# GpSimd's scatters spaced in the plan, first fetches on its queue, ten result tiles: a polysketch attention with a top-2 router on one core

## The chip, the cores and the metric

One core of a Trainium2 chip runs the whole kernel in one launch. The metric is the device time of that launch in microseconds (us). "TensorE" (PE in the profile) multiplies matrices, "VectorE" (DVE), "ScalarE" (ACT) and "GpSimd" (POOL) work on elements, "SyncE" (SP) only issues transfers. Every engine runs its own list of instructions in order and waits on semaphores for the others.

## What is computed

Everything is float32. q, k and v have 4 batches, 4 heads, 1088 tokens and 32 values a head; S1 and S2 are 8 x 32 sketches. phi(x) is the outer product of two sketches of x, 64 features:

```python
def phi(x):
    a = np.einsum('rd,bhsd->bhsr', S1, x)
    b = np.einsum('rd,bhsd->bhsr', S2, x)
    return np.einsum('bhsi,bhsj->bhsij', a, b).reshape(*x.shape[:-1], r * r)
q_p, k_p = (phi(q), phi(k))
kv = np.einsum('bhsf,bhsd->bhfd', k_p, v)
z = np.sum(k_p, axis=2)
num = np.einsum('bhsf,bhfd->bhsd', q_p, kv)
den = np.einsum('bhsf,bhf->bhs', q_p, z)[..., None] + 1e-06
attn = num / den
```

The attention's result is read as x, 4352 tokens of 128 values, and goes through a router with 8 experts:

```python
noisy_logits = x @ w_gate + np.log1p(np.exp(x @ w_noise)) * noise
top2 = np.argpartition(-noisy_logits, 2, axis=1)[:, :2]
top2_w = softmax over the two chosen logits
for e in range(8):
    for k in range(2):
        mask = top2[:, k] == e
        h = np.maximum(x[mask] @ w1[e], 0.0)      # w1[e]: 128 x 1024
        out[mask] += top2_w[mask, k, None] * (h @ w2[e])   # w2[e]: 1024 x 128
```

## The kernel before, in words

**A plan orders everything.** Every step is a `Job` in a `Plan`: an engine (or a choice of ScalarE and VectorE), an estimated cost, what it reads and writes, a priority and, for a transfer, a size. `Plan.order()` (L86) is a greedy list scheduler that simulates the engines and, of the jobs that can start soonest (within `SOON`), takes the one with the lowest priority number. `Plan.write()` (L150) emits the jobs in that order. So the plan's times only decide the *order* of each engine's list; on the chip the engines run their lists as fast as the real waits let them. A tile tag has so many buffers (`tag(name, bufs, ...)`), and a job that opens a new buffer waits, in the plan and on the chip, for the users of the one that it replaces. A job with `paced` starts in the plan no sooner than 7.0 us (`SPAN`) after the fifth paced job before it (`BURST`).

**Attention.** For each batch b, `load_kq` and `load_v` issue the loads on SyncE; `turned` transposes k and q on VectorE into kT and qT (L549, L551); `features` multiplies them with the sketches on TensorE (L571), then ScalarE or VectorE copies the low part (lo), VectorE adds it (ab, L590) and forms the outer products phk and phq (L605). GpSimd copies v into vaug (L618, L621). TensorE sums k features times v (L642). `queries` transposes phq on TensorE (L687), copies that to pT, multiplies with the folded weights (L698), and VectorE divides (den, L713; x, L705) and sums the gates' logits. kT, qT, vld, phk, phq and vaug have one buffer each, kq two.

**Router.** It works in five waves: wave 0 is the first four chunks of 128 tokens of b = 0, wave 1 the rest of b = 0, and waves 2, 3, 4 are b = 1, 2, 3. VectorE chooses the experts, counts on TensorE give every token its place, VectorE weighs the rows with their gate into xg (L915), and GpSimd scatters each chunk with an indirect transfer into the table xs in DRAM (L778, out `xs`, 129 values a row: 128 of x and the number of the pair): 8 scatters in wave 0, 10 in wave 1, 18 in each later wave. Between two scatters of one kind `pool_scatter` sets a one-element memset (L776). The table's unused rows are cleared in nine transfers on SyncE (`xs<-pad`).

**Blocks.** 48 blocks u follow, each with one expert and 128 rows (n = 1) or 256 (n = 2) of the table. The first three (`DIRECT`) get their rows by a product with one-hot tiles `oh` (L973). The next five (u < 8, `QUICK`) fetch xb on ScalarE's queue and are transposed by TensorE; the later ones fetch xb in four pieces and the pair numbers ix on SyncE, and VectorE transposes (bT, L1005). A block needs all scatters of its wave and of the one before. Then TensorE multiplies with w1 into hp (L1015, two buffers), ScalarE makes h = relu(hp) (L1023), TensorE multiplies with w2 into acc (L1030), ScalarE or VectorE copies that to `y` (five buffers), and GpSimd scatters y to the table `pairs` (L778, out `pairs`), at places read from first_at, xb or ix. `sums` at last reads both rows of a token from `pairs`, adds them (L1078) and writes out.

**Zero products.** At the end `idle` fills the plan's gaps of TensorE in the first 60 us with products of a tile of zeros, `zb` (L1247).

The priorities that matter here: TOP is -1000, block products have 1000 + 100u, the router of batch b has some 100 b + 20, and the xs scatters one more than that.

Of the kernel before, what the change touches and what calls it, by code (L numbers as in the profile page):

```python
# [29 lines left out]
class Job:  # L30
    def __init__(self, engines, cost, emit, lat, prio, size):
        self.engines, self.cost, self.emit, self.lat, self.prio, self.size = engines, cost, emit, lat, prio, size
        self.paced = False
        self.deps, self.opens, self.end, self.done = set(), [], None, None


class Plan:
# [6 lines left out]
    BURST, SPAN = 5, 7.0  # L44
# [41 lines left out]
    def order(self):  # L86
        free, done, moved, paced, lanes = {}, [], 0.0, [], []
        left = {j: len(j.deps) for j in self.jobs}
        after = {j: [] for j in self.jobs}
        for j in self.jobs:  # L90
            for d in j.deps:
                after[d].append(j)
        cand = [j for j in self.jobs if not left[j]]
        number = {j: i for i, j in enumerate(self.jobs)}

        def ready(j, e):

            return max((d.end if d.engine == e and d.size is None else d.done for d in j.deps), default=0.0)

        while cand:  # L100
            starts = []
            for j in cand:
                at = 0.0
                for b in j.opens:
                    bufs, _, used = self.tags[b.tag]
                    if b.placed or len(used) < bufs:
                        continue
                    ends = [x.done for x in used[-bufs].users]
                    if None in ends:
                        at = None  # L110
                        break
                    at = max(at, max(ends))
                if at is None:
                    continue
                if j.size is not None:
                    if "SP" in j.engines:
                        at = max(at, moved - self.AHEAD)
                    if len(lanes) >= self.LANES:
                        at = max(at, lanes[-self.LANES])
                if j.paced and len(paced) >= self.BURST:  # L120
                    at = max(at, paced[-self.BURST] + self.SPAN)
                for e in j.engines:
                    starts.append((max(at, free.get(e, 0.0), ready(j, e)), j, e))
            assert starts, [(j.engines, j.prio, [b.tag for b in j.opens]) for j in cand]
            first = min(x[0] for x in starts)
            _, s, _, j, e = min((j.prio, s, number[j], j, e) for s, j, e in starts if s <= first + self.SOON)
            cand.remove(j)
            cost = j.cost[e] if isinstance(j.cost, dict) else j.cost
            j.start, j.end, j.engine = s, s + cost, e
            free[e] = j.end  # L130
            if j.paced:
                paced.append(s)
            j.done = j.end + j.lat + self.SYNC
            if j.size is not None:
                moved = max(moved, j.end + 0.6) + j.size / self.RATE
                j.done = max(j.done, moved + 0.8 if e == "SP" else j.end + 1.4 + 2 * j.size / self.RATE)
                lanes.append(j.done)
            j.opens = [b for b in j.opens if not b.placed]
            for b in j.opens:
                b.placed = True  # L140
                self.tags[b.tag][2].append(b)
            done.append(j)
            for a in after[j]:
                left[a] -= 1
                if not left[a]:
                    cand.append(a)
        assert len(done) == len(self.jobs)
        return done
# [13 lines left out]
def kernel(  # L162
# [27 lines left out]
    C = 8  # L190
# [59 lines left out]
    tag("b2", 2, [P, 4 * H, R])  # L250
# [22 lines left out]
    tag("y", 5, [P, 2 * D])  # L273
    tag("oh", 2, [P, 4, P])
# [23 lines left out]
    ROWS = 1.0  # L298
    LAND = 2.2
# [6 lines left out]
    def dma(q, o, i, r, w, prio, size=0, issue=0.45, after=(), done=None):  # L306

        eng = {"SP": Y, "ACT": A}
# [5 lines left out]
        return add(q, issue, emit, r=r, w=w, prio=prio, lat=LAND, after=after, size=size)  # L314
# [7 lines left out]
    def load_kq(b, which, prio):  # L322
# [3 lines left out]
        dma("SP", lambda: t.t[:], lambda: pairs_of(src[b]), (), [t], prio, size=557e3)  # L326

    def load_v(b, prio, queues=("SP",)):
# [3 lines left out]
        for l in range(4):  # L332
            dma(queues[l % len(queues)], lambda l=l: t.t[32 * l:32 * l + 32, :, 0:C, :].rearrange("p h c d -> p h (c d)"),
                lambda l=l: src[:, :, C * l:C * l + C, :].rearrange("t h c d -> t h (c d)"),
                (), [(t, l)], prio, size=131e3, issue=1.2)
# [69 lines left out]
    def constants():  # L405
# [12 lines left out]
        pool_job(1.2, 4, lambda: G.memset(vaug[:, :, :, DH:2 * DH], 0.0), ["ones_v"])  # L418
# [64 lines left out]

    def decode_job():
# [7 lines left out]
        def turns(e):  # L492
            for i in range(2):
                T.transpose(ps.t[:, 2 * R * i:2 * R * i + 2 * R], shared["s4"][:, i, :, :].rearrange("r h d -> r (h d)"),
                            ident[0:2 * R, 0:2 * R])
# [59 lines left out]
    def features(jobs, prio, whole=False, after=(), first=None):  # L555

# [6 lines left out]
        def emit(e):  # L563
            for i, (xT, t, _) in enumerate(jobs):
                lhsT = xT.t[:, P * t:min(P * t + P, S)]
                if whole:
                    for c in range(2):
                        T.matmul(ps.t[rows, W * i:W * i + W], lhsT=lhsT, rhs=sk[:, c, :, :].rearrange("p h x -> p (h x)"),
                                 start=(c == 0), stop=(c == 1), skip_group_check=True)
                else:  # L570
                    T.matmul(ps.t[rows, 2 * W * i:2 * W * i + 2 * W], lhsT=lhsT,  # L571
                             rhs=sk[:].rearrange("p c h x -> p (c h x)"), start=True, stop=True)
        last = add("PE", n * (0.3 if whole else mm(128)), emit, lat=0.15, r=["sk"] + [(xT, t // 4) for xT, t, _ in jobs],
                   w=[ps], prio=prio if first is None else first, touch=[dst for _, _, dst in jobs], after=after)
        if whole:
            b2 = new("b2")
            add(EV, either(n * H * R), lambda e: copy(
                e, b2.t[rows, 0:n * H, :], ps.t[rows, 0:W * n].rearrange("p (i w r) -> p i w r", w=2, r=R)[:, :, 1, :]),
                r=[ps], w=[b2], prio=prio)

            def factors(i, m, w):
                if w == 0:
                    return ps.t[rows, W * i:W * m].rearrange("p (i w r) -> p i w r", w=2, r=R)[:, :, 0, :]
                return b2.t[rows, H * i:H * m, :]
            source = (ps, b2)
        else:
            lo, ab = new("lo"), new("ab")
            x4 = lambda: ps.t[rows, 0:2 * W * n].rearrange("p (i c y) -> p i c y", i=n, c=2)
            add(EV, either(W * n), lambda e: copy(e, lo.t[rows, 0:n, :], x4()[:, :, 1, :]), r=[ps], w=[lo], prio=prio)
            add("DVE", vec(W * n), lambda e: V.tensor_tensor(  # L590
                out=ab.t[rows, 0:n * H, :, :].rearrange("p (i h) w r -> p i (h w r)", h=H),
                in0=x4()[:, :, 0, :], in1=lo.t[rows, 0:n, :], op=ALU.add), r=[ps, lo], w=[ab], prio=prio)

            def factors(i, m, w):
                return ab.t[rows, H * i:H * m, w, :]
            source = (ab,)
        i = 0
        while i < n:
# [10 lines left out]
            add("DVE", vec(256 * (m - i)), product, r=list(source), w=[(jobs[i][2], jobs[x][1]) for x in range(i, m)], prio=prio)  # L609
# [5 lines left out]
    def keys_values(b, prio, head=False, after=()):  # L615
# [8 lines left out]
        features([(kT, t, pk) for t in range(4)], prio + 1, False, after)  # L624
# [3 lines left out]
        features([(kT, t, pk) for t in range(4, 8)], prio + 2, False, after)  # L628
        if head:
            features([(kT, C, pk)], prio + 3, False, after)  # L630
        else:
            features([(kT, C, pk), (qT, C, pq)], prio + 3, False, after)
        turned(qT, qld, 0, 4, prio + 3)
        features([(qT, t, pq) for t in range(4)], prio + 4, False, after, prio + 2.9)
# [39 lines left out]
        features([(qT, t, pq) for t in range(4, 8)], prio + 6, False, after)  # L674
# [107 lines left out]
    def router(b, t0, n, w, x, lg, prio):  # L782
# [153 lines left out]
        for t in range(n):  # L936
            rows = slice(0, HB if t0 + t == C else P)
            for i in range(2):
# [8 lines left out]
                pair.paced = w > 0  # L947
# [10 lines left out]
    def block(u, w, e, r, n):  # L958
# [5 lines left out]
        if u < DIRECT:  # L964
            oh = new("oh")
# [11 lines left out]
        else:  # L977
# [9 lines left out]
            if u < QUICK:  # L987
                dma("ACT", lambda: xb.t[:, 0:n, :], lambda: rows.rearrange("(c p) x -> p c x", p=P),
                    there, [xb], -10 + u, size=66e3 * n, issue=0.5, done=done)
# [45 lines left out]
        for c in range(n):  # L1035
# [8 lines left out]
            sent = add("POOL", ROWS + 0.3, emit, r=[y, xb if u < QUICK else ix], w=[key], prio=TOP + u, lat=LAND)  # L1044
            sent.paced = True
# [7 lines left out]
    def first_index(prio):  # L1053

        def done(ins):
# [4 lines left out]
        dma("ACT", lambda: first_at[:].unsqueeze(2), lambda: xs_e[0:DIRECT, 0:P, D:XW].rearrange("e p x -> p e x"),  # L1060
            routed[0], ["first_at"], prio, issue=0.5, done=done)
# [176 lines left out]
    began = [None]  # L1238

    def idle(a, b):  # L1240
# [3 lines left out]
        if began[0] is None:  # L1244
            began[0] = tile_now("hp")
        for _ in range(int((b - a - 0.3) * 0.8 / (0.44 if b < 7.5 else 0.22))):
            T.matmul(began[0][:], lhsT=zb[:, 0:P], rhs=zb[:], start=True, stop=True)  # L1247
# [37 lines left out]
```

## Time and profile before

| | us |
|---|---|
| median of three runs | 415.56 (410.94 to 416.64) |
| profiled execution, whole time | 407.02 |
| its span in the trace | 405.3 |
| last matmul ends | 392.3 |
| TensorE busy | 355.4 |
| GpSimd busy | 174.3 |
| VectorE busy | 148.7 |
| ScalarE busy | 137.9 |
| TensorE clock granted, mean | 0.954 |

The profile comes from one execution, 407.02 us long, of which the trace shows 405.3. The page gives busy time by engine, the span in 40 slices, the transfer queues, the chain of work that ended last, and groups of instructions: line, engine, operation, output and inputs, count, busy time, mean of one, and the idle time ahead with the engine that ended it. In a timeline each row has a start, a duration, the engine and the line; in brackets stands how long the engine was idle before it and what released it. `remote` is a release that the trace can't put down to an instruction, `issue` time in which it waited for nothing that the trace shows. "SPq" and "ACTq" are the transfer queues that SyncE and ScalarE issue on.

Runs of matmuls are merged into one row, so that the start of a next row can lie a little ahead of the end of the last.

### The profile page before, as it was taken

The page shows a single profiled execution, that of the slowest core. Times are in us where ns is not written, and L with a number is a line of the kernel's source. Part 1 is how long each engine was busy: PE and PEld are TensorE (multiplying, and loading weights), DVE is VectorE, ACT ScalarE, POOL GpSimd, SP SyncE. Part 2 cuts the span into 40 slices and gives each one's busy share as a digit, 9 for nine tenths or more (in the row PEclk, how much of TensorE's full clock was granted, in tenths as well). Part 3 has the DMA queues.
Part 4 walks back from the last instruction along what each step waited for, and adds up shares of the span by engine and source line. Part 5 has one row for each costly group of instructions (what it writes and reads, how often), then busy time and mean ns, then how long its engine had stood idle before and what let it go on. Part 6 is the DMA issues. An engine that isn't in the chain of part 4 may idle for free.

```text
span 405.3 us, 7333 instructions
## 1 busy us (share of the span) xinstructions
PE 355.4 (88%) x2562; PEld 323.4 (80%) x2562; DVE 148.7 (37%) x559; ACT 137.9 (34%) x284; POOL 174.3 (43%) x333
## 2 busy tenths in 40 slices
PE   7988799369998989857996999999999999999970
PEld 4857689269997988747996898899898998999960
DVE  6687565077884777215770000200000110001101
ACT  1252352124532263112541333433334333333430
POOL 6826203572277647680254566522323224233230
PEclk9999899869999999979997999999999999999995
DMA  6988966744231115411121223622212511115403
GB/s 169 278 275 264 290 193 171 258 145 123 37 71 43 45 37 91 84 49 21 31 57 39 52 59 62 198 46 39 42 26 48 180 30 34 22 27 156 121 12 89
DMA packets 68767, 40.69 MB, mean 100 GB/s; under 512 B 49767, under 2 KB 61193, under 8 KB 68728
## 3 DMA queue, kind: packets, MB, share of 16 engines
q1 hardware_dynamic: 62360, 30.24, 30.5%
q0 software_dynamic: 4608, 8.96, 6.9%
q10 hardware_dynamic: 1760, 1.01, 1.1%
q8 instruction: 21, 0.34, 0.4%
q14 instruction: 18, 0.15, 0.1%
HBM read 24.24 MB, written 16.19 MB: 100 GB/s over the span
## 4 chain that ended last, share of the span: by engine, by line
issue 35%; POOL 24%; PE 23%; DMA 9%; DVE 3%; SPq 3%; ACT 1%; POOLq 1%; another core or an unknown queue 1%; DVEq 0%; ACTq 0%
POOL pairs L778 12%; POOL xs L778 8%; PE hp L1015 6%; PE acc L1030 5%; PE bank L571 4%; DMA kq<-in_k_dram 3%; PE bank L698 3%; SPq L311 3%; DMA xb<-xs 2%; DMA pairs<-y,ix 2%; DMA pr<-pairs 2%; POOL step L776 1%; PE bank L687 1%; PE acc L642 1%; PE bank L642 1%
## 5 line engine op out<-in xcount | busy, mean ns | idle before, releaser
L1030 PE MATMUL acc<-w2s,h 128*128 128x128 f32 x1152 | 154.0, 283 | 6.8 <-ACT h L1023 4.6
L1030 PEld LDWEIGHTS acc<-w2s,h 128*128 128x128 f32 x1152 | 144.4, 194 | 18.7 <-ACT h L1023 9.0
L1015 PE MATMUL hp<-bT,w1s 128*128 128x128 f32 (+1 forms) x768 | 147.4, 334 | 2.6 <-ACT h L1023 1.4
L778 POOL DMA_INDIRECT pairs<-y,ix x64 | 63.1, 987 | 143.3 <-ACT y L304 129.2
L1015 PEld LDWEIGHTS hp<-bT,w1s 128*128 128x128 f32 x768 | 115.3, 195 | 10.9 <-ACT h L1023 1.8
L1023 ACT ACTIVATE h<-hp 128x512 f32<-128x512 f32 x141 | 83.9, 597 | 108.2 <-PE hp L1015 78.9
L778 POOL DMA_INDIRECT xs<-xg,to x72 | 72.5, 1007 | 40.9 <-issue 15.7
L1005 DVE STREAM_TRANSPOSE bT<-xb 128x256 f32<-128x256 f32 (+1 forms) x40 | 15.6, 390 | 138.5 <-PE hp L1015 115.7
L304 ACT COPY y<-acc 128x128 f32<-128x128 f32 (+1 forms) x48 | 15.4, 320 | 65.1 <-PE acc L1030 53.0
L698 PE MATMUL bank<-kvw,pT 128*128 128x98 f32 x144 | 20.1, 290 | 9.0 <-issue 4.9
L698 PEld LDWEIGHTS bank<-kvw,pT 128*128 128x128 f32 x144 | 18.5, 203 | 10.3 <-issue 5.8
L687 PE MATMUL bank<-ident,phq 128*128 128x128 f32 x72 | 11.9, 294 | 12.3 <-DVE phq L605 10.8
L304 ACT COPY pT<-bank 128x512 f32<-128x512 f32 (+1 forms) x18 | 10.0, 562 | 34.0 <-PE bank L687 15.9
L1078 DVE TENSOR_TENSOR o<-pr 128x512 f32<-128x512 f32 (+2 forms) x12 | 6.7, 558 | 36.8 <-DMA pr<-pairs 34.4
L687 PEld LDWEIGHTS bank<-ident,phq 128*128 128x128 f32 x72 | 8.8, 153 | 13.4 <-issue 11.9
L304 ACT COPY lo<-bank 128x256 f32<-128x256 f32 (+2 forms) x21 | 7.1, 337 | 20.1 <-PE bank L571 13.2
L642 PE MATMUL bank<-phk,vaug 128*128 128x128 f32 (+1 forms) x108 | 13.1, 277 | 0.0
L605 DVE TENSOR_TENSOR phq<-ab 128x512 f32<-128x512 f32 (+1 forms) x20 | 12.9, 669 | 0.3
L571 PE MATMUL bank<-sk,kT 128*128 128x128 f32 (+1 forms) x72 | 12.5, 322 | 0.5 <-DVE sk L499 0.5
L642 PEld LDWEIGHTS bank<-phk,vaug 128*128 128x128 f32 (+1 forms) x108 | 12.5, 191 | 0.4
L605 DVE TENSOR_TENSOR phk<-ab 128x512 f32<-128x512 f32 (+1 forms) x20 | 12.6, 646 | 0.3
L571 PE MATMUL bank<-sk,qT 128*128 128x128 f32 (+1 forms) x72 | 11.5, 299 | 0.2 <-issue 0.2
(153 smaller groups left out, 242.8 us busy)
## 6 DMA issues: line engine op xcount, KB each, us to landing
xs<-pad SPq DMA_DIRECT2D x9, 516.0 KB
w1s<-in_moe_w_dram SPq DMA_DIRECT2D x8, 512.0 KB
w2s<-in_moe_w_dram SPq DMA_DIRECT2D x8, 512.0 KB
xb<-xs SPq DMA_DIRECT2D x96, 32.0 KB
pr<-pairs SPq DMA_DIRECT2D x6, 512.0 KB
kq<-in_k_dram SPq DMA_DIRECT2D x4, 544.0 KB
kq<-in_q_dram SPq DMA_DIRECT2D x4, 544.0 KB
vld<-in_v_dram SPq DMA_DIRECT2D x14, 128.0 KB
```

Of the source, the lines that this page charges most:

```text
L304: A.copy(o, i) if e == "ACT" else V.tensor_copy(o, i)
L311: ins = eng[e].dma_start(o(), i())
L571: T.matmul(ps.t[rows, 2 * W * i:2 * W * i + 2 * W], lhsT=lhsT, rhs=sk[:].rearrange("p c h x -> p (c h x)"), start=True, stop=True)
L605: V.tensor_tensor(out=jobs[i][2].t[rows, jobs[i][1]:jobs[m - 1][1] + 1, :, :].rearrange("p c h (i j) -> p (c h) i j", i=R), in0=factors(i, ...
L642: T.matmul(kvp.t[:, P * a:P * a + P], lhsT=va.t[0:K, t, hs, :].rearrange("p h d -> p (h d)"), rhs=pk.t[0:K, t, hs, :].rearrange("p h f -> ...
L687: T.transpose(ps.t[:, c0:c0 + P], pq.t[:, t + i, 2 * a:2 * a + 2, :].rearrange("p h f -> p (h f)"), ident[:])
L698: T.matmul(ps2.t[:, c0:c0 + 2 * YW], lhsT=pT.t[:, P * (2 * i + a):P * (2 * i + a) + P], rhs=kvw.t[:, a, :], start=True, stop=True)
L778: return G.indirect_dma_start(**kw)
L1005: add("DVE", vec(P * n), lambda _: V.transpose(bT.t[:, 0:P * n], flat()), r=[xb], w=[bT], prio=TOP + u)
L1015: T.matmul(hp.t[:, P * n * i:P * n * (i + 1)], lhsT=w1s[:, e, P * (js * g + i):P * (js * g + i + 1)], rhs=bT.t[:, 0:P * n], start=True, st ...
L1023: A.activation(out=h.t[:], in_=hp.t[:], func=AF.Relu)
L1030: T.matmul(acc.t[:, D * c:D * c + D], lhsT=h.t[:, P * (n * i + c):P * (n * i + c + 1)], rhs=w2s[:, e, j, :], start=(j == 0 and c == 0), st ...
```

## The change

1. The plan's `BURST` and `SPAN` go. `paced` is a number: a paced job starts in the plan at least so long after the last paced one, 1.45 us for the scatters of wave 0 and 1.7 us for all others and for the result scatters. `far` marks them: a job on the same engine that depends on one waits in the plan for its landing, not only for its end.
2. The result scatters' priority goes from TOP + u to 400 + 0.01u, which puts them behind the xs scatters of the wave that is routed at that time.
3. The five xb fetches of blocks 3 to 7 and first_at go from ScalarE's queue to GpSimd's. Transfers of GpSimd no longer count among the plan's eight `LANES`.
4. Ten buffers of `y` instead of five. The one-hot tiles `oh` are taken from `o`. An unused branch (`whole`, `b2`) goes.
5. The plan adds `MARGIN`, 6.0 us, to the landing of the loads of k, q and v of batches 2 and 3.
6. Zero products: ten at the start, one between the two transposes of the sketches, one in each later gap before 7.5 us; in the later gaps the share of the gap that they fill goes from 0.8 to 0.85. The memset of vaug's upper half moves ahead on GpSimd.

GpSimd's list, which follows from 1 to 3: 8 scatters of wave 0, the six fetches, 10 scatters of wave 1 (7, the small copy of vaug for b = 2, 3, the large copy), 9 result scatters, 18 of wave 2 (7, a copy, 1, a small copy, 10), 6 results, 18 of wave 3, 4 results, 18 of wave 4, then the results that are left. Before, results stood among the scatters of a wave, two results and three xs scatters in turn, for example. On VectorE the transposes of batch 2's k go behind the phq, den and x of batch 1; on SyncE three pieces of v stand ahead of batch 2's k instead of one, and the five ix loads ahead of batch 3's k. Lines of the changed kernel are 6 to 9 lower than before: the scatters are L772, h is L1017, the w2 products L1024.

```diff
-    BURST, SPAN = 5, 7.0
...
-            return max((d.end if d.engine == e and d.size is None else d.done for d in j.deps), default=0.0)
+            return max((d.end if d.engine == e and d.size is None and not d.far else d.done for d in j.deps), default=0.0)
...
-                    if len(lanes) >= self.LANES:
+                    if "POOL" not in j.engines and len(lanes) >= self.LANES:
                         at = max(at, lanes[-self.LANES])
-                if j.paced and len(paced) >= self.BURST:
-                    at = max(at, paced[-self.BURST] + self.SPAN)
+                if j.paced and paced:
+                    at = max(at, paced[-1] + j.paced)
...
-                lanes.append(j.done)
+                if e != "POOL":
+                    lanes.append(j.done)
+                j.done += j.margin
...
-    tag("y", 5, [P, 2 * D])
-    tag("oh", 2, [P, 4, P])
+    tag("y", 10, [P, 2 * D])
...
+    MARGIN = 6.0
...
-        dma("SP", lambda: t.t[:], lambda: pairs_of(src[b]), (), [t], prio, size=557e3)
+        dma("SP", lambda: t.t[:], lambda: pairs_of(src[b]), (), [t], prio, size=557e3, margin=MARGIN if b > 1 else 0.0)
...
-        pool_job(1.2, 4, lambda: G.memset(vaug[:, :, :, DH:2 * DH], 0.0), ["ones_v"])
+        pool_job(1.2, 0.5, lambda: G.memset(vaug[:, :, :, DH:2 * DH], 0.0), ["ones_v"])
...
             for i in range(2):
+                if i:
+                    T.matmul(warm()[:, 0:2 * P], lhsT=zb[:, 0:P], rhs=zb[:, 0:2 * P], start=True, stop=True)
                 T.transpose(ps.t[:, 2 * R * i:2 * R * i + 2 * R], shared["s4"][:, i, :, :].rearrange("r h d -> r (h d)"),
...
-                pair.paced = w > 0
+                pair.paced, pair.far = 1.45 if w == 0 else 1.7, True
...
-            oh = new("oh")
+            oh = new("o")
...
-                dma("ACT", lambda: xb.t[:, 0:n, :], lambda: rows.rearrange("(c p) x -> p c x", p=P),
-                    there, [xb], -10 + u, size=66e3 * n, issue=0.5, done=done)
+                dma("POOL", lambda: xb.t[:, 0:n, :], lambda: rows.rearrange("(c p) x -> p c x", p=P),
+                    there, [xb], -10 + u, size=66e3 * n, issue=1.0, done=done)
...
-            sent = add("POOL", ROWS + 0.3, emit, r=[y, xb if u < QUICK else ix], w=[key], prio=TOP + u, lat=LAND)
-            sent.paced = True
+            sent = add("POOL", ROWS + 0.3, emit, r=[y, xb if u < QUICK else ix], w=[key], prio=400 + 0.01 * u, lat=LAND)
+            sent.paced, sent.far = 1.7, True
...
-        dma("ACT", lambda: first_at[:].unsqueeze(2), lambda: xs_e[0:DIRECT, 0:P, D:XW].rearrange("e p x -> p e x"),
-            routed[0], ["first_at"], prio, issue=0.5, done=done)
+        dma("POOL", lambda: first_at[:].unsqueeze(2), lambda: xs_e[0:DIRECT, 0:P, D:XW].rearrange("e p x -> p e x"),
+            routed[0], ["first_at"], prio, issue=1.0, done=done)
...
-        for _ in range(int((b - a - 0.3) * 0.8 / (0.44 if b < 7.5 else 0.22))):
-            T.matmul(began[0][:], lhsT=zb[:, 0:P], rhs=zb[:], start=True, stop=True)
+        n = 10 if a == 0 else 1 if b < 7.5 else int((b - a - 0.3) * 0.85 / 0.22)
+        for _ in range(n):
+            T.matmul(warm()[:], lhsT=zb[:, 0:P], rhs=zb[:], start=True, stop=True)
```

## The prediction

> **What bounds the kernel now.** I read the page first, then the chain of waits, then TensorE's timeline around each of its pauses, and last the timelines of the engines that it paused for.
>
> ```profile
> PE 355.4 (88%) x2562; PEld 323.4 (80%) x2562; DVE 148.7 (37%) x559; ACT 137.9 (34%) x284; POOL 174.3 (43%) x333
> issue 35%; POOL 24%; PE 23%; DMA 9%; DVE 3%; SPq 3%; ACT 1%; POOLq 1%; another core or an unknown queue 1%; DVEq 0%; ACTq 0%
> ```
>
> TensorE is busy for 355.4 of 405.3 us, so the other 49.9 us are all that an edit of order can win; part of them is the tail (the last matmul ends at 392.3, 13 us before the end) and the start. The stages differ (columns: stretch, its length, then busy time of TensorE, of its weight loads, VectorE, ScalarE and GpSimd, granted clock, DMA share, GB/s):
>
> ```profile
> 72.00:92.00 20.00, 9.63 (x76) 9.24 (x76) 8.53 (x23) 4.27 (x11) 12.92 (x21) 0.74 0.62 194
> 154.00:187.00 33.00, 25.49 (x171) 22.31 (x170) 11.75 (x32) 7.56 (x16) 22.53 (x37) 0.90 0.37 70
> 208.00:225.00 17.00, 13.89 (x74) 12.28 (x74) 3.98 (x14) 4.50 (x9) 10.07 (x15) 0.80 0.23 52
> 260.00:380.00 120.00, 120.00 (x829) 110.09 (x828) 10.45 (x26) 46.07 (x85) 35.64 (x68) 1.00 0.28 64
> ```
>
> From 260 to 380 TensorE is never idle and at full clock: there the change can win nothing. The loss is before 260, in two kinds of place. The first, in the timelines of TensorE, of VectorE and of SyncE's queue:
>
> ```profile
> 74.24 0.38 PE L687 MATMUL bank<-ident,phq 128*128 128x128 f32 x2
> 84.99 1.09 PE L687 MATMUL bank<-ident,phq 128*128 128x128 f32 x4 [10.37 <-DVE phq L605]
> 85.87 1.92 PE L1015 MATMUL hp<-bT,w1s 128*128 128x128 f32 x8
> ...
> 81.81 1.30 DVE L551 STREAM_TRANSPOSE kT<-kq 128x512 f32<-128x512 f32 x2 [13.52 <-DMA kq<-in_k_dram]
> ...
> 59.30 8.53 SPq L311 DMA_DIRECT2D xs<-pad  x5
> 67.94 1.28 SPq L311 DMA_DIRECT2D vld<-in_v_dram  x1
> 69.31 2.03 SPq L311 DMA_DIRECT2D kq<-in_k_dram  x1
> ```
>
> TensorE stands 10.37 us for phq of batch 1. VectorE could have made it, but ahead of that in its order stand the transposes of batch 2's k, and they wait 13.52 us for a load that SyncE issued only at 69.31, behind five clears; it landed 12.5 us later. After the stop the matmuls run at half speed (eight of L1015 take 1.71 us to the next start, against 0.89 at full clock).
>
> The second kind of place is GpSimd's runs of scatters, here ScalarE, TensorE and GpSimd:
>
> ```profile
> 218.12 0.60 ACT L1023 ACTIVATE h<-hp 128x512 f32<-128x512 f32 x1 [3.70 <-remote]
> ...
> 218.77 2.08 PE L1030 MATMUL acc<-w2s,h 128*128 128x128 f32 x8 [3.11 <-ACT h L1023]
> ...
> 213.29 0.97 POOL L778 DMA_INDIRECT xs<-xg,to  x1 [0.30 <-issue]
> ...
> 215.82 0.96 POOL L778 DMA_INDIRECT xs<-xg,to  x1 [0.23 <-issue]
> ```
>
> The first products of that block ended at 214.77, so ScalarE could have made h then; it began at 218.12, 1.34 us after the seventh scatter of an unbroken run had ended (216.78). Outside such runs the hand-over from hp to h takes 0.04 to 0.10 us; at a fifth scatter it is 0.55, further on in a run 1.3 to 4.7. So long runs of scatters, 1.27 us apart, hold up TensorE's signals. What TensorE lost (idle time, plus the extra of half-clock rows after it): run of 8 from 33.3: 3.8 us; 7 from 115.8: 1.7; 8 from 154.3: 1.1; 13 from 166.8: 9.3; 7 from 208.1: 6.2. Together 22.1 us for 18 scatters past the fifth of their run, 1.23 us each. Runs of five with pauses of 1.8 us between (231 to 257) cost three stops of 0.32 to 0.38, about 1 us.
>
> **Part by part, against the profiled execution's 407.02 us.**
>
> *Later k loads (MARGIN).* The plan now believes that batch 2's k lands 6 us later, and in VectorE's order its transposes go behind batch 1's phq, gates and x. TensorE no longer waits there: between its last transposes of phq C and its first product that needs batch 2's kT stand, priced by the same groups at full clock, 0.44 + 0.89 + 1.31 + 0.44 + 0.89 + 0.11 + 1.79 + 0.87 + 0.87 + 0.89 + 1.76 = 10.3 us, so it arrives there at 74.62 + 10.3 = 84.9. The load itself gets later: two more pieces of v stand ahead of it on SyncE, 1.28 us each by the row above, so it lands at 81.81 + 2.6 = 84.4 at worst; 1.30 us of transposes make 85.7. Left is a stop of 0.8 (0 if the pieces cost the load nothing, 1.5 if VectorE adds 0.7). Half-clock time falls away too: 0.44 + 0.81 + 0.29 = 1.5 us on the rows from 84.99 to 89.19. Sum: -10.4 - 1.5 + 0.8 = **-11.1** (-10.4 to -11.9). Behind the moved transposes VectorE's last den and x of batch 1 wait, and on them the router of wave 1, but by the same 0.8 at most.
>
> *Runs of scatters.* Pacing is a matter of the plan; nothing on GpSimd waits for it. What decides is GpSimd's new order. Result scatters had the first priority and now have one behind the wave's xs scatters. Wave 1: 7 xs, a copy of vaug, 3 xs. Then nine results. Wave 2: 7, a copy, 1, a small copy, 10. Six results. Waves 3 and 4: 18 unbroken each, with four results between. Before, waves 2, 3 and 4 lost 2.3, 10.4 and 7.5 us, together 20.2. Nearest rows for after: wave 2 as a run of 7 (1.7) and one of 8 (3.8), 5.5; wave 3, one run of 18 where there were 8 and 13 with results among them, again 10.4; wave 4 as wave 3. That is 26.3, so +6.1 at this reading; 0 if the waves just keep their 20.2. I take the middle, **+3**: fewer scatters lie in the same stretch, since results go elsewhere. The bounds: all three waves as cheap as wave 2 was, -13.3; above, in waves 3 and 4 everything past the fifth scatter is lost (13 x 1.27 = 16.5 us, and 3 us at half clock as after 217), 9.8 + 2 x 19.5 - 20.2 = +28.6. Deferring results needs the ten y tiles, and frees an ix tile later, and SyncE's xb loads stand behind the ix load; five fetched blocks of about 7.3 us each cover that. Without that cover a late block costs what is missing of the 2 to 3 us of a landing.
>
> *Fetches on GpSimd's queue.* Five xb and first_at leave ScalarE, where they took 0.35 us each and first_at 2.36, with y waiting 2.14 behind it. No plain fetch on GpSimd is in this trace; the nearest rows are ScalarE's 0.35 and GpSimd's own scatters, 0.96 to 1.0 us, and I take the latter, the same engine: 6 us in all. They lie in its own idle time: after the wave's last scatter (42.69 + 0.96) it does nothing until 60.93:
>
> ```profile
> 42.69 0.96 POOL L778 DMA_INDIRECT xs<-xg,to  x1 [0.23 <-issue]
> 49.19 0.22 POOL L908 COPY xg<-pid 128x18 int32<-128x18 int32 x1 [5.54 <-DMA xs<-xg,to]
> ...
> 60.93 1.31 POOL L778 DMA_INDIRECT xs<-xg,to  x1 [11.51 <-DVE xg L915]
> ```
>
> The fetch needs the landing (49.19), and six issues end near 55.2, before 60.93: cost **0**, up to +1 if six issues in a row act like a run of six. If the cover were gone, 6 us would delay wave 1's scatters. The Trainium skill ("SBUF — State Buffer", "SBUF: two separate sides") speaks against it: descriptors of a transfer issued on GpSimd are written by GpSimd, which is locked out while VectorE runs a two-port operation, and its example goes from 620 to 3100 ns. By that rule six issues would take up to 18.6 us, an estimate from that page, end near 68 instead of 55, and make the sum about +7 worse; no row here shows VectorE holding an issue of GpSimd, so I go by the rows.
>
> *Start.* Ten zero products instead of nine (0.447 us each, so the tenth ends at 5.87 beside a transpose that ran at 5.69: +0.2), one more between the two sketch transposes, one or none before 7.5 us, to have the clock up sooner. Sixteen L571 take 3.78 us there against two times 0.89 to 1.06 later. But VectorE and ScalarE carry that stretch: **-0.6** (+0.2 to -0.9). The earlier memset of vaug on GpSimd (1.02 us) delays ident, which is needed only at 5.69: nothing.
>
> *Dead code, oh tiles from o:* nothing; no row exists for the removed branch.
>
> Sum: -11.1 + 3 + 0 - 0.6 = **-8.7**, 398.3. The median before, 415.56, is 1.021 times the profiled time; the same factor gives 406.7.
>
> **Rivals.**
> 1. *Slower: unbroken runs hold TensorE's signals.* Price by the mean, 1.23 us for each scatter past the fifth: wave 2 has 2 + 6, waves 3 and 4 have 13 each, 34 x 1.23 = 41.8 against 20.2: +21.6. With -11.1 - 0.6 it is +9.9, 416.9, or **425.6**. For it: the run of 13 and the run of 8 are in one wave and still cost 9.3. Against: the run of 8 at 154 cost 1.1, where TensorE had other work ready. It decides from +20 in this term (2% is 8.3 us of 415.56).
> 2. *Nothing left:* k lands later than worked out (three v pieces on the same DMA engines at 194 GB/s), half of the stop returns (+5), and the waves cost +6.1: -0.6, **about 415**. Against: the trace puts only 1.28 us on a piece.
> 3. *More than forecast:* every wave runs beside ready matmuls as wave 2 did, -13.3 for +3: 382.0, **390.0**. For it: PE at 0.97 busy between 226 and 262 with xs scatters in runs of five; against: runs are longer now.
> That the change does not do what it says is part of rival 1: spacing in the plan is no spacing on the chip.
>
> **How the numbers follow.** Forecast 0.52 (its own range 397 to 412; 0.32 of it below 407.2, which is 2% faster, about what a measurement can tell from no change, and 0.20 above); rival 1 0.30; rival 2 0.08 (0.06 within 2%, 0.02 slower); rival 3 0.10. So faster 0.42, same 0.26, slower 0.32. The range reaches from the forecast's low end to the far side of rival 1, 397 to 428; left out are rival 3 and the dearest of rival 1.
>
> **What would show it.** TensorE's 10.37 us before L687 gone and the clock in 72 to 92 near 1; six fetch issues on GpSimd between 49 and 56; in the stretches of waves 3 and 4 the idle time of TensorE behind `remote` waits of ScalarE, 10 us each by the forecast, 16 to 19 by rival 1. I am wrong if batch 2's k becomes a stop of over 3 us, or if h is not late in runs of 18.

## The result, and the profile after

The changed kernel takes 437.87 us (median of 4 runs, 435.58 to 439.19) against 413.25 us of the kernel before in the same comparison (4 runs, 407.46 to 416.64): a ratio of 1.070, with a 95% interval of 1.058 to 1.081. Ratios leave out executions that are over 1.5% above the fastest of their kernel on that chip (here 415.56 and 416.64 of the kernel before), and so do the times of the fourth and fifth group below; other times are medians of all executions. It is slower by 7%, where 406.7 us, 2% faster, was forecast; the range ended at 428. The profiled execution took 435.58 us, 28.6 more than that of before, with a span of 433.9 us.

The page's first row and the chain that ended last:

```profile
PE 360.0 (83%) x2564; PEld 326.2 (75%) x2564; DVE 148.3 (34%) x561; ACT 137.8 (32%) x282; POOL 179.8 (41%) x367
...
PE 29%; issue 24%; DMA 12%; another core or an unknown queue 12%; POOL 10%; SPq 9%; DVE 2%; ACT 1%; POOLq 1%; ACTq 0%; DVEq 0%
```

TensorE's idle time is 433.9 - 360.0 = 73.9 us, against 49.9 before: 24.0 more. Its busy time is 4.6 us longer at a lower clock (granted 0.921 on the mean, against 0.954). Together these are the 28.6 us. On the chain an entry has gone from 1% to 12%: "another core or an unknown queue", a release that the trace cannot place.

The stretches (columns as before, with the length of the stretch first: busy time of TensorE, of its weight loads, VectorE, ScalarE, GpSimd, then granted clock, DMA share, GB/s):

```profile
72.00:92.00 20.00, 18.10 (x158) 17.51 (x158) 14.99 (x53) 9.67 (x19) 10.83 (x21) 1.00 0.50 147
126.00:154.00 28.00, 17.48 (x127) 16.78 (x126) 12.56 (x68) 8.12 (x18) 9.71 (x20) 0.76 0.19 36
154.00:187.00 33.00, 21.05 (x154) 18.81 (x152) 10.61 (x29) 5.55 (x12) 23.85 (x42) 0.84 0.30 64
225.00:260.00 35.00, 17.02 (x75) 14.17 (x76) 0.45 (x1) 4.29 (x9) 21.73 (x41) 0.71 0.17 45
```

In 72 to 92, where TensorE had been busy for 9.63 us at a clock of 0.74, it now is for 18.10 at 1.00: the stop for batch 1's phq is gone, as forecast. But from 126 on TensorE is idle for a third to a half of three stretches, and in 225 to 260 only GpSimd is busy for more than half of the time. This is what ScalarE and TensorE wait for there, and what GpSimd does meanwhile (timelines of the three):

```profile
224.47 0.60 ACT L1017 ACTIVATE h<-hp 128x512 f32<-128x512 f32 x1 [1.67 <-PE hp L1009]
232.30 0.37 ACT L305 COPY y<-acc 128x256 f32<-128x256 f32 x1 [7.23 <-remote]
237.30 0.60 ACT L1017 ACTIVATE h<-hp 128x512 f32<-128x512 f32 x1 [4.63 <-remote]
244.99 0.60 ACT L1017 ACTIVATE h<-hp 128x512 f32<-128x512 f32 x1 [7.08 <-issue]
252.78 1.09 ACT L1017 ACTIVATE h<-hp 128x512 f32<-128x512 f32 x2 [7.20 <-remote]
...
226.12 1.89 PE L1009 MATMUL hp<-bT,w1s 128*128 128x256 f32 x8
237.95 2.07 PE L1024 MATMUL acc<-w2s,h 128*128 128x128 f32 x8 [9.95 <-issue]
245.63 2.08 PE L1024 MATMUL acc<-w2s,h 128*128 128x128 f32 x8 [3.90 <-ACT h L1017]
...
218.70 1.15 POOL L772 DMA_INDIRECT xs<-xg,to  x1 [0.96 <-DVE xg L909]
239.03 0.90 POOL L772 DMA_INDIRECT xs<-xg,to  x1 [0.22 <-issue]
247.93 0.97 POOL L772 DMA_INDIRECT pairs<-y,ix  x1 [0.23 <-issue]
```

The second group of four matmuls in the first TensorE row ended at 228.01; ScalarE's h for it starts at 244.99, 17 us later, though ScalarE had little else to do (it was idle for 7.08 us just before). GpSimd meanwhile ran 24 scatters without a break (218.70 to 248.9): 17 of xs and then 7 results, whose y had long been ready. The other long runs are 14 (117 to 135) and 20 (161 to 187). TensorE stood 10.5, 15.6 and 18.2 us in and just behind the three. In the other direction nothing is late: h ends at 237.90 and TensorE starts on it at 237.95.

### The profile page after: what moved, and what is told of

Same layout as the page of the kernel before. It is cut to its first block, busy times and chain, and to the rows that moved or that the text cites. A ratio compares the mean times of both kernels' runs of the same rounds, so it can differ in the third digit from the quotient of the medians.

```text
span 433.9 us, 7359 instructions
## 1 busy us (share of the span) xinstructions
PE 360.0 (83%) x2564; PEld 326.2 (75%) x2564; DVE 148.3 (34%) x561; ACT 137.8 (32%) x282; POOL 179.8 (41%) x367
## 4 chain that ended last, share of the span: by engine, by line
PE 29%; issue 24%; DMA 12%; another core or an unknown queue 12%; POOL 10%; SPq 9%; DVE 2%; ACT 1%; POOLq 1%; ACTq 0%; DVEq 0%
PE acc L1024 11%; PE hp L1009 10%; SPq L312 9%; POOL pairs L772 8%; DMA xs<-pad 3%; PE bank L692 3%; DMA vld<-in_v_dram 3%; DMA pairs<-y,xb 2%; DMA pairs<-y,ix 1%; PE bank L578 1%; PE bank L681 1%; PE bank L636 1%; PE acc L636 1%; DMA pr<-pairs 1%
## 5 line engine op out<-in xcount | busy, mean ns | idle before, releaser
L1024 PE MATMUL acc<-w2s,h 128*128 128x128 f32 x1152 | 156.2, 285 | 20.7 <-issue 12.1
L1024 PEld LDWEIGHTS acc<-w2s,h 128*128 128x128 f32 x1152 | 145.5, 196 | 33.5 <-ACT h L1017 15.5
L772 POOL DMA_INDIRECT pairs<-y,ix x64 | 63.1, 986 | 167.7 <-ACT y L305 133.1
L1017 ACT ACTIVATE h<-hp 128x512 f32<-128x512 f32 x140 | 83.4, 597 | 127.0 <-PE hp L1009 86.1
L772 POOL DMA_INDIRECT xs<-xg,to x72 | 72.7, 1009 | 46.9 <-DVE xg L909 17.6
L999 DVE STREAM_TRANSPOSE bT<-xb 128x256 f32<-128x256 f32 (+1 forms) x40 | 15.6, 391 | 164.1 <-PE hp L1009 109.8
L305 ACT COPY y<-acc 128x256 f32<-128x256 f32 (+1 forms) x47 | 15.1, 320 | 70.2 <-PE acc L1024 52.7
L692 PE MATMUL bank<-kvw,pT 128*128 128x98 f32 x144 | 21.4, 307 | 8.8 <-ACT pT L305 8.8
L692 PEld LDWEIGHTS bank<-kvw,pT 128*128 128x128 f32 x144 | 20.7, 223 | 9.2 <-ACT pT L305 9.0
L305 ACT COPY pT<-bank 128x512 f32<-128x512 f32 (+1 forms) x18 | 10.0, 562 | 21.7 <-PE bank L681 10.7
L1238 PE MATMUL hp<-zb 128*128 128x512 bf16 x35 | 11.2, 466 | 1.4 <-POOL zb L409 1.4
L770 POOL MEMSET step<- 1x1 f32 x136 | 12.1, 89 | 0.1
```

The lines of the kernel that those rows point to most:

```text
L305: A.copy(o, i) if e == "ACT" else V.tensor_copy(o, i)
L692: T.matmul(ps2.t[:, c0:c0 + 2 * YW], lhsT=pT.t[:, P * (2 * i + a):P * (2 * i + a) + P], rhs=kvw.t[:, a, :], start=True, stop=True)
L770: G.memset(step[:, 0:1], 0.0)
L772: return G.indirect_dma_start(**kw)
L999: add("DVE", vec(P * n), lambda _: V.transpose(bT.t[:, 0:P * n], flat()), r=[xb], w=[bT], prio=TOP + u)
L1017: A.activation(out=h.t[:], in_=hp.t[:], func=AF.Relu)
```

## The experiments

Two theories. **Runs**: GpSimd's unbroken runs of scatters hold back TensorE's signals, rival 1 of the prediction, dearer than it was priced. **Order**: the deferred results, the fetches on GpSimd's queue or the moved loads make the stops. The kernels came to five chips in five groups, each with the kernel before beside it; ratios are against that, and only kernels of one group are compared in us, except where two chips are set against each other.

### First group: each part, and real pauses

**Margin alone**, on the kernel before: the `MARGIN` lines of the diff and nothing else.

> The kernel before with the 6 us margin on the loads of batches 2 and 3 alone. If the stop of 10.37 us for phq is worth what it seems, TensorE does not stand there any more and the time falls by 10 to 12 us against before (413 to about 402). Rival: the stop only moves (k lands later, or the waves' scatters bunch up instead), then the time stays within 4 us of before.

Measured: 415.45 us beside 412.5, ratio 1.010 (0.993 to 1.028): no gain, where 10 to 12 us were expected, and no clear loss. TensorE's stop of 10.37 us is gone, its largest between 65 and 90 us is 1.50. But the new order put 14 scatters in a row twice, at 107 and at 170, and TensorE stood 8.0 and 10.7 us in and just behind them, most of the first here:

```profile
128.09 0.99 PE L667 MATMUL bank<-wg,kvT 33*64 33x49 f32 x8 [7.83 <-ACT kvT L306]
```

The rival's second clause was right: the scatters bunch up, and by these stops the gain went into longer runs.

**Results first again**, in the changed kernel:

```diff
-            sent = add("POOL", ..., prio=400 + 0.01 * u, lat=LAND)
+            sent = add("POOL", ..., prio=TOP + u, lat=LAND)
```

> The changed kernel with the result scatters' old priority, so that they stand among the xs scatters again. Theory 'runs' (unbroken runs of GpSimd's scatters hold back TensorE's signals): runs get short except one of 12, and the 44 us that TensorE stands between 120 and 255 us fall to 10 to 15, time 405 to 412. Rival 'fetches' (the six fetches on GpSimd's queue, or the ten y tiles, cost the time): 430 to 438, as the changed kernel.

Measured: 401.86 us, ratio 0.982 (0.972 to 0.992). One priority takes the ratio from 1.070 to 0.982; the time is 3 us below the range that "runs" gave. TensorE's idle time between 120 and 255 us falls from 44.3 to 17.3 us (10 to 15 expected). The longest run is 13 scatters (151 to 167), and TensorE's one great stop ends just behind it:

```profile
170.19 1.12 PE L681 MATMUL bank<-ident,phq 128*128 128x128 f32 x4 [10.90 <-DVE kvw L305]
```

**Real pauses**, with the order on every engine as in the changed kernel (the memsets stand ahead of the fifth scatter, so the first stretch has four):

```diff
+    rest = const.tile([P, 48], F32, name="rest")
+    in_row = [0]
...
         last_on_pool[0] = kind
+        if kind == "rows":
+            in_row[0] += 1
+            if in_row[0] % 5 == 0:
+                for _ in range(8):
+                    G.memset(rest[:], 0.0)
```

> The changed kernel with the same order on every engine, but after every fifth xs scatter GpSimd sets a small tile eight times, about 2.4 us without a scatter. Theory 'runs': stops over 5 us behind late ScalarE starts vanish, TensorE's idle time between 120 and 255 us falls from 44 to under 12 us, time 398 to 410 although GpSimd does 30 us more. Rival 'order' (the deferred results, their y and ix tiles or the late loads make the stops): time stays at 438 or rises by some of the pauses.

Measured: 406.47 us, ratio 0.991 (0.986 to 0.996). Eight memsets take 1.53 us, not 2.4 (GpSimd, between the fifth and the sixth scatter):

```profile
169.94 0.96 POOL L779 DMA_INDIRECT xs<-xg,to  x1 [0.22 <-issue]
...
170.92 1.53 POOL L778 MEMSET rest<- 128x48 f32 x8
172.61 0.96 POOL L779 DMA_INDIRECT xs<-xg,to  x1 [0.15 <-issue]
```

Inside runs of five TensorE lost at most 1.4 us; what was left came behind mixed runs of xs scatters and results of 6, 8 and 12, which the pauses did not split (3.2, 4.1 and 6.0 us). So the time lies in the range expected, but the idle time between 120 and 255 us is 16.2 us and not under 12, and one stop of over 5 us is left. GpSimd does more, no engine's order moves, and the ratio falls from 1.070 to 0.991: on this chip the runs are the cause, not the order as such.

**Fetches back on ScalarE's queue**, in the changed kernel (`"POOL"` to `"ACT"`, issue cost 0.5):

> The changed kernel with the six first fetches on ScalarE's queue again. Theory 'runs': the runs of 18 remain, time 430 to 440. Rival 'fetches': the time falls back to 410 to 418.

Measured: 441.5 us, ratio 1.080 (1.068 to 1.091), no better than the changed kernel's 1.070. The fetches are not the cause.

### Second group: pauses everywhere

The count now takes in both kinds of scatter, in four kernels:

```diff
         last_on_pool[0] = kind
+        in_row[0] += 1
+        if in_row[0] % 5 == 0:
+            for _ in range(8):
+                G.memset(rest[:], 0.0)
```

> The changed kernel with eight small memsets (1.5 us) after every fifth scatter of either kind. The run before with pauses among the xs scatters alone kept stops of 3.1, 3.4 and 6.1 us, each behind a mixed run of 6, 8 and 12. Theory 'runs': those go too, time 393 to 399. Rival 'the later results make those stops': it stays within 3 us of 406.

> The changed kernel with the result scatters' old priority and the pauses after every fifth scatter of either kind. Theory 'runs': the stops of 3.2 and 11.3 us behind the runs of 8 and 13 and the half-clock time after them go, 402 becomes 386 to 392. Rival 'bank or kv dependence makes the 11.3 us stop': 400 to 404.

> The kernel before with the pauses alone. Theory 'runs': its own stops in waves 2 to 4 (20 us worked out) mostly go, the stop of 10.4 us for batch 2's k stays: 392 to 400 against 412. Rival 'only runs over 13 matter': 408 or more.

> The kernel before with the margin and the pauses. If the margin is worth its 11 us once no run gives them back, this is 9 to 13 us faster than the kernel before with pauses alone. Rival 'the load's stop only moves': the two agree within 3 us.

| beside 413.78 us | us | ratio |
|---|---|---|
| changed, pauses | 393.64 | 0.952 (0.944 to 0.960) |
| changed, results first, pauses | 384.96 | 0.930 (0.922 to 0.938) |
| before, pauses | 394.53 | 0.953 (0.944 to 0.962) |
| before with margin, pauses | 388.13 | 0.937 (0.930 to 0.945) |

All went the way that "runs" said, two of them inside its ranges (393.64 and 394.53), one 1 us below (384.96). The fourth missed: the margin was to win 9 to 13 us, and the rival said under 3. The changed kernel loses 11% of its time by pauses alone (0.952 / 1.070 = 0.89). The kernel before with pauses keeps its stop for batch 2's k, here 12.39 us:

```profile
82.46 1.08 PE L689 MATMUL bank<-ident,phq 128*128 128x128 f32 x4 [12.39 <-DVE phq L607]
```

The margin takes it away, and is worth 394.53 - 388.13 = 6.4 us, between the two, about half of the stop: some of the time comes back in stops of 1.4 to 2.0 us at 82, 94, 98 and 101.

### Third group: doses of pause, and a surprise

All with results first; two memsets after every scatter, four after every fifth, one after every fifth, and the eight of before with `MARGIN = 0.0`.

> As the run with results first and pauses (385), but two small memsets (0.38 us) after every scatter instead of eight after every fifth: scatters 1.65 us apart on the chip. Theory 'backlog' (each scatter leaves some 1.4 us of work behind that TensorE's signals queue with; at 1.27 us apart it piles up, at over 1.44 it does not): h is never over 0.3 us late and the time is 377 to 384. Rival 'count' (five scatters with no other break of 1 us make the hold, however they are spaced): runs of 18 stay runs, 398 to 440.

> As the run with results first and pauses, with four memsets (0.76 us) after every fifth scatter. Backlog: five scatters pile up 5 x 0.15 = 0.75 us, so this just suffices, 384 to 388. If a pause must be over 1 us to count at all: 396 to 404.

> The same with one memset (0.19 us) after every fifth scatter. Backlog: 0.15 us less in five of 0.75, so runs still hold the signals: 395 to 402. Rival 'any other instruction resets it': 384 to 388.

> The run with results first and pauses, with the margin on the loads set to 0. If the margin takes the stop for batch 2's k away also here, this is 7 to 12 us slower than 385 and shows a stop of about 10 us before phq's transposes near 80 us; if the new order alone does it, the same within 2 us.

Measured: 378.23, 376.98, 378.17 and 380.34 us; ratios 0.994 (0.990 to 0.997), 0.992 (0.988 to 0.995), 0.992 (0.988 to 0.996) and 1.000 (0.997 to 1.003). The kernel before itself took 380.65 us on this chip (31 runs, 378.8 to 382.9), not 412. And with one memset after every fifth scatter, a run of 13 scatters cost nothing. The stretch of that run, first in the results-first kernel of the first group's chip, then in the one-memset kernel of this chip:

```profile
150.00:172.00 22.00, 9.81 (x74) 8.88 (x74) 5.25 (x12) 2.95 (x8) 13.45 (x24) 0.78 0.47 82
```

```profile
146.00:168.00 22.00, 22.00 (x172) 20.61 (x172) 14.20 (x48) 8.17 (x18) 16.18 (x31) 1.00 0.54 93
```

GpSimd's scatters lie 1.27 us apart in both, 1.31 where the one memset stands. TensorE is busy 9.81 us of 22 in the one and 22.00 of 22 in the other, with no h later than 0.51 us in the whole second kernel. So the hold, as this delay of TensorE's signals is called from here on, looked like a matter of the chip, and the doses had told nothing, since there was nothing to cure. Without the margin (the last of the four) TensorE stopped for 3.60 us for phq at 76, not for 10, and the time was 2 to 3 us over the other three; as these have other pauses, that is no clean price of the margin.

### Fourth group: the same doses where the hold exists

> The changed kernel, on another chip. If the hold belongs to the chip: where the kernel before takes about 412, this takes 434 to 442; where that takes about 381, the runs of 14 to 24 cost nothing, no ScalarE start is over 1 us late, and this takes 372 to 380. If the hold comes from the program alone: slower by 5 to 8% on either.

> Results first and two small memsets after every scatter (1.65 us apart). Where the hold exists: backlog says 377 to 384 beside 412 (8% faster); count says 398 to 440. Where it doesn't: 377 to 380 beside 381.

> Results first and four memsets (0.76 us) after every fifth scatter. Where the hold exists: backlog 384 to 390 beside 412, a needed pause of over 1 us 396 to 404. Where it doesn't: 375 to 379 beside 381.

> Results first and one memset (0.19 us) after every fifth scatter. Where the hold exists: 395 to 402 beside 412. Where it doesn't: 376 to 380 beside 381.

On this chip the kernel before took 410.2 us. The distances in the table are the traces' own, from the start of one scatter of a run to the next. They are shorter than the expectations had reckoned: behind two memsets 1.50 us instead of 1.65, behind four 1.89, behind one 1.31, since a part of the memsets falls into the gap of 0.31 us that lies behind a scatter anyway. Two scatters of the kernel with two memsets:

```profile
151.00 0.96 POOL L778 DMA_INDIRECT xs<-xg,to  x1 [0.59 <-issue]
...
152.50 0.96 POOL L778 DMA_INDIRECT xs<-xg,to  x1 [0.16 <-issue]
```

| beside 410.2 us | mean distance of scatters in a run | us | ratio |
|---|---|---|---|
| changed kernel | 1.27 us | 434.74 | 1.063 (1.053 to 1.073) |
| results first, one memset after five | (4 x 1.27 + 1.31)/5 = 1.28 | 399.18 | 0.974 (0.965 to 0.982) |
| results first, four after five | (4 x 1.27 + 1.89)/5 = 1.39 | 383.38 | 0.934 (0.928 to 0.940) |
| results first, two after each | 1.50 | 380.74 | 0.929 (0.922 to 0.936) |

The one-memset kernel is 21 us slower than on the other chip, by the same instructions: h is up to 8.1 us late here. Between a mean of 1.28 and one of 1.39 us 15.8 us are won; from there to 1.50 it is 2.6 more. "Count" falls: a run of ten scatters 1.50 us apart, with no other break, leaves TensorE nearly undisturbed (spaced kernel, stretch of that run):

```profile
150.00:172.00 22.00, 20.21 (x150) 18.58 (x150) 12.96 (x45) 9.68 (x19) 17.16 (x54) 1.00 0.44 81
```

"Backlog" stands as the better description. The first profile of the changed kernel bears it out in one more place. Behind its runs of 14, 20 and 24, which end at 135.15, 186.76 and 248.90, ScalarE's held work starts at 137.41, 189.76 (ScalarE, below) and 252.78 (above): 2.26, 3.00 and 3.88 us later, 0.15 to 0.16 us for each scatter of the run.

```profile
137.41 0.58 ACT L305 COPY pT<-bank 128x512 f32<-128x512 f32 x1 [9.42 <-remote]
...
189.76 0.37 ACT L305 COPY lo<-bank 128x256 f32<-128x256 f32 x1 [9.65 <-remote]
```

On the fourth group's chip the same three runs give 2.24, 2.99 and 3.90. This is what has piled up if a scatter leaves 1.42 us of work and the next comes after 1.27. It is not a full description: some signals came through in the middle of a run (the starts at 232.30, 237.30 and 244.99 above), and at 1.50 us five h still start 0.9 to 2.0 us late, where it said 0.3 at most. Another reading of the four rows was not tested: that a long enough gap from the end of a scatter to the start of the next lets the signals through. The gaps are 0.31 us without memsets, 0.35 behind one, 0.54 behind two and 0.93 behind four.

### Fifth group: what the rest is worth without the hold

Two memsets after every scatter, in the changed kernel and in the kernel before.

> The changed kernel with two small memsets after every scatter, 1.65 us apart. Without the hold, the prediction's other terms (-11.1 for the load, -0.6 for the start) should show against the kernel before with the same spacing: 382 to 388. Rival 'the deferred results bunch up and cost by themselves': 390 or more.

> The kernel before with two small memsets after every scatter. The stop of 10 us for batch 2's k stays, the rest of its holds goes: 388 to 396, 6 to 12 us over the changed kernel with the same spacing. If the load's stop hides elsewhere: the two within 3 us.

This chip too is one without the hold (before: 380.57 us). Measured: 379.74 and 384.76 us, ratios 0.998 (0.994 to 1.001) and 1.010 (1.006 to 1.013). Both are 2 to 3 us below what was written down, which reckoned with the other kind of chip. The spacing costs the kernel before 4 us where it cures nothing. The rest of the change wins 384.76 - 379.74 = 5.0 us, less than the 6 to 12 expected. TensorE's stops that differ, in the kernel before with spacing and in the changed one with spacing:

```profile
80.06 1.09 PE L689 MATMUL bank<-ident,phq 128*128 128x128 f32 x4 [10.71 <-DVE phq L607]
```

```profile
53.30 0.48 PE L993 MATMUL turn<-ident,xb 128*128 128x128 f32 x1 [3.01 <-DMA xb<-xs]
...
97.43 3.40 PE L1015 MATMUL hp<-bT,w1s 128*128 128x128 f32 x16 [5.86 <-DVE mk L847]
```

10.71 us go, and so do 3.73 at 151.09 for a block's rows; 3.01 (0.69 in the kernel before) and 5.86 come. The first of these is for a fetched xb, now issued by GpSimd. The second is named after VectorE's mk, but what made VectorE late is a block's rows:

```profile
96.97 0.31 DVE L1005 STREAM_TRANSPOSE bT<-xb 128x128 f32<-128x128 f32 x1 [6.33 <-DMA xb<-xs]
```

## Why the prediction was wrong

- **The step that failed is the term of the runs**, +3 in the sum. Between 120 and 255 us, where the three long runs lie, TensorE's idle time went from 135.00 - 119.34 = 15.7 us to 135.00 - 90.68 = 44.3 (rows below: the kernel before, then the changed one). That is +28.7, with half-clock time on top; the term's upper bound was +28.6. I had the price, 1.23 us for each scatter past the fifth of its run, and the mechanism, rival 1. Then the forecast took "the middle, +3", made from whole waves of the kernel before instead of from that price. In the profile after the three long runs have 9 + 15 + 19 = 43 scatters past the fifth, and TensorE stood 44.3 us about them: 1.03 each, and half-clock time besides, which the price of 1.23 had in it. So the price was about right; the sum went without it.

```profile
120.00:255.00 135.00, 119.34 (x847) 108.74 (x846) 55.76 (x222) 44.44 (x89) 75.83 (x122) 0.95 0.26 55
```

```profile
120.00:255.00 135.00, 90.68 (x615) 83.08 (x614) 50.93 (x210) 32.52 (x65) 65.78 (x120) 0.82 0.20 43
```

- **The count was short as well.** I wrote "waves 3 and 4 have 13 each". The results stored up during a wave come at its end, all ready, and joined it: 17 + 3 and 17 + 7 in one run. Likewise 11 + 3 in wave 2, which I had split by a copy. Deferring results lengthens the very runs that it was meant to leave alone. So even rival 1, at 425.6, fell short.
- **"Fewer scatters lie in the same stretch"**, my reason for the low value, was no reason: what counts is how many follow each other in a run, and how closely, as the doses show.
- **The load of batch 2's k** came out as forecast, but in part by another path. The stop of 10.37 us became none (0.70 at 87.18), and the clock in 72 to 92 went from 0.74 to 1.00. I had the load 2.6 us later; in fact SyncE issued it 7.6 us sooner, at 61.68 instead of 69.31, since its five clears began at 50.20 instead of 59.30, and VectorE transposed at 77.03 without a wait (SyncE in the changed kernel, below). Why SyncE got there sooner stays open. VectorE's new order alone suffices: in the kernel with the margin alone the load goes out at 69.52, and the stop is gone too. The earlier load without the margin still leaves a stop, of 3.60 us. Its worth as a time was smaller than forecast: 6.4 us with pauses on a chip with the hold, 5.0 for all of the rest of the change on a chip without, instead of 11.1 and 11.7. A part comes back as a stop at 97 us, in the spaced kernel for block rows, which I had counted as covered by five fetched blocks.

```profile
50.20 7.85 SPq L312 DMA_DIRECT2D xs<-pad  x5
...
61.68 1.35 SPq L312 DMA_DIRECT2D kq<-in_k_dram  x1
```

- **The fetches** cost GpSimd nothing, as forecast: 2.72 us for five and 0.76 for first_at, in its idle time before the next scatter at 59.52 (GpSimd in the changed kernel, below). Not foreseen is that the rows came later, and TensorE waited 3.01 us for the first (in the spaced run).

```profile
48.65 2.72 POOL L312 DMA_DIRECT2D xb<-xs  x5 [6.96 <-DMA xs<-xg,to]
51.36 0.76 POOL L312 DMA_DIRECT2D first_at<-xs  x1
```

- **The rule of the Trainium skill** ("SBUF — State Buffer", "SBUF: two separate sides"), by which a two-port operation of VectorE holds up transfers issued on GpSimd, was not put to the test: the five issues took 0.54 us each while VectorE worked, but the trace does not tell which of its operations use both ports. Moving the fetches back to ScalarE's queue made the kernel no faster (ratio 1.080 against 1.070).
- **The start**: -0.6 forecast. Sixteen L571 fell from 3.78 to 2.09 us (L578 after), and the first counting product ran at 25.86 instead of 27.82: -2.0 in these two executions. But the kernel before with pauses, its start unchanged, reached that product at 25.84 too; over all runs it came between 25.84 and 27.82 us with the old start and between 25.61 and 27.43 with the new one. So no gain is shown.
- **Rivals 2 and 3** played no part: k came sooner, not later, and the waves lost more than before, not less.

Not settled: what it is that holds TensorE's signals. The trace shows a release without a source, and the transfers of GpSimd's queue take as long on both kinds of chip: in the one-memset kernel 7.6% of 376.8 us on the one and 7.1% of 402.7 on the other, 28.6 us both times. Nor is it settled that the chip as such decides: none of the five chips was met in a second group, so something that lasts for a group's runs on a chip would look the same. Nor was the changed kernel without spacing run on a chip without the hold; by the last group (0.998 against 1.010) it would be about 1% faster than before there, but that is argued, not shown.

## What to carry to other kernels

Look for a consumer that starts late although its producer has long ended, and see what runs unbroken on GpSimd at that time; on the chips that have this hold, a mean of 0.12 us more per scatter won 5% of the kernel's time here (results first, ratio 0.982 to 0.934). Spacing in a plan orders a queue and does not space it: if a distance matters, put real instructions there, and count every kind of work that will be ready when the run begins. Of the versions tried, results first with four small memsets after every fifth scatter, or two after every one, beats the kernel before on either kind of chip: 6.6 and 7.1% faster where the hold exists, 0.8 and 0.6% where it does not.

## What the runs showed of the hardware

- One program had two times on different chips: the kernel before took 410.6 to 413.8 us on three chips and 380.6 on two others, with the same instructions. The one-memset kernel took 399.18 us on one chip and 378.17 on another. Each of the five chips was met in one group only.
- The difference shows in TensorE's signals while GpSimd issues scatters 1.27 us apart: on the one kind of chip h is up to 17 us late (a run of 24), in the one-memset kernel 8.1 us; in the same kernel on the other kind 0.5 us at most.
- On the first kind a mean distance of 1.39 us removes most of it (h at most 2.5 us late) and 1.28 little.
- On the first kind ScalarE's held work starts 0.15 to 0.16 us per scatter behind the end of runs of 14, 20 and 24.
- Signals towards TensorE are not held: TensorE starts 0.05 us after h in the run of 24.
